# Second batch's scores stored ahead in DRAM, and the first batch's softmax divided after the product with V

## The chip, the cores and the metric

The kernel runs on one core of a Trainium2 chip. The metric is device time in microseconds: 1224.6 us, the median of three runs (1224.48 to 1224.6).

## The reference, cut to what matters

Attention over 4 batches, 8 heads, 576 tokens, head dimension 64, where each query keeps its 32 largest scores; then two MLPs of width 512 and hidden width 2048 over the 2304 tokens. Q, K, V and the result are float32, the MLP weights 64-bit; the kernel works with float32 operands, most of them split into a high and a low part.

```python
scores = scale * np.matmul(q, k.transpose(0, 1, 3, 2))
kth = np.partition(scores, -top_k, axis=-1)[..., -top_k:-top_k + 1]
scores = np.where(scores >= kth, scores, -1e9)
attn = np.exp(scores - max); attn = attn / (np.sum(attn) + 1e-09)
x = np.matmul(attn, v)              # 2304 x 512 after the heads are joined
x = np.square(np.maximum(x @ w_in, 0)) @ w_out
h = x @ w_in2; out = np.maximum(0.01 * h, h) @ w_out2
```

## The kernel before, in words

**Units and tiles.** The tokens of a batch are cut into units (UNITS): batch 0 into 256, 256 and 64 tokens, batches 1 to 3 into 256 and 320 each. For each of the four head pairs a unit gives tiles of 128 query rows by 576 keys: 144 tiles, 36 a batch, worked on in 72 pairs. The order is batch 0 (tiles 0 to 35), batch 1 (36 to 71: the 256-token unit up to 51, then the 320-token one), then batches 2 and 3 (72 to 143).

**One tile.** Scores (L278): 2 or 4 matmuls for each of two halves of 288 keys, each half evicted by ScalarE (L279). VectorE finds the 32 largest in four MAX8 (L800) with three MATCH_REPLACE8 between (L802). ScalarE and GpSimd drop what lies below (L297, L298), ScalarE takes exp with its row sum (L302), GpSimd and VectorE form the reciprocal `rc` (L306, L307), and ScalarE multiplies the tile by it (`norm`, L311). TensorE transposes the tile (`pt_main` L316, `pt_left` L329 for the last 64 keys), ScalarE evicts, and TensorE multiplies with V. Batch 0 (the units below NATIVE = 3) does this in plain float32 (`av`, L377); the others, for which `split(uh)` is true, with a high and a low part of the transposed tile (PTs, VT, L321, L322, L388). `x_out` (L397 on) writes the high and low part of the result into the MLP's input (L405, L408).

**MLP blocks.** The tokens go through the MLP in blocks of 512, 256, 384, 512, 256 and 384. Block 0 is the first two units, block 1 needs the first unit of batch 1, block 2 all of batch 1, block 3 the first units of batches 2 and 3. Blocks 0 to 3 run both layers as soon as they are ready. Block 0 also converts the weights, which come as 64-bit words: two ScalarE copies (L485, L486), two VectorE operations (L490, L491), a high part (L495) and a low part on GpSimd (L498), and a store to DRAM (L506, L507). Later blocks load the converted weights (L514, L515).

**Scores made ahead.** For a batch in EARLY (2 and 3) the scores are not made just before they are used. They are made during the first batch, into `stage` tiles through PSUM tiles `sp`, and stored to DRAM (`sd`, L282); `load_s` (L286) brings a tile back 24 slots before its pair starts. Their K is split by GpSimd (L117, L240: `st["i"]` is 99 there, so `split_hi` never picks ScalarE, as it does for batches 0 and 1, L115), their Q by ScalarE or GpSimd and GpSimd (L257). The K, Q and `stage` tiles lie in a pool `ahead`, the PSUM tiles in `stage_psum`; both are closed by `open_mlp`, and the MLP's own pools take that memory and those banks.

**What sets the order.** The work is emitted by slots, 16 to a pair of tiles. In each slot stand VectorE's next top-k instruction, the functions that `at(slot, ...)` put there, and a share of MLP matmuls: `rate` is a block's groups of three matmuls over the slots until the next block is ready; what is left when the next block is ready is emitted before that block. Direct scores stand 30 slots ahead of their pair (DLEAD). The ahead scores are spread over the slots of FILL, 2 to 245. Block 0 is ready at slot 274, block 1 at 434. The framework's scheduler keeps each engine's instructions in an order near that of emission and puts in the semaphores; each engine then runs its own list in order, and SP issues all loads and stores but those of the result.

Of the kernel before, what the change touches and what calls it, by code (L numbers as in the profile page):

```python
# [8 lines left out]
F = mybir.dt.float32  # L9
R = mybir.dt.float32r  # L10
U = mybir.dt.uint32
AF = mybir.ActivationFunctionType
OP = mybir.AluOpType
# [23 lines left out]

SPILL = 128

NATIVE = 3  # L40

EARLY = (2, 3)
FILL = (2, 245)
KPB = 2
NST = 3
SDB = 2
# [24 lines left out]
def topk_attention_moe_moe2_kernel(  # L71
# [11 lines left out]
    D = v.shape[-1]  # L83
    P = 128
# [8 lines left out]
    PE, ACT, DVE, POOL, SP = nc.tensor, nc.scalar, nc.vector, nc.gpsimd, nc.sync  # L93
# [9 lines left out]
    ident = const.tile([P, P], F, tag="ident", name="ident")  # L103
# [23 lines left out]
    for u in units:  # L127
        for hp in range(NHP):
            n = u["n"]
            uh = dict(u=u, hp=hp, n=n, b=u["b"], first=(u["t0"] == 0), ti=len(tiles), idx=len(uhs),  # L130
                      c0=P * (hp % 2) if n == 64 else 0)
# [14 lines left out]
    def direct(uh):  # L146
        return uh["b"] not in EARLY

# [3 lines left out]
    def split(uh):  # L152
        return uh["u"]["i"] >= NATIVE

# [5 lines left out]
    for i in range(4):  # L160
        x = const if i < 2 else ahead
# [10 lines left out]
    spill = const.tile([P, NHP, SPILL], F, tag="spill", name="spill")  # L172
    early_ctx = ExitStack()
    early = early_ctx.enter_context(tc.tile_pool(name="early", bufs=1))
    PT = early.tile([P, 5, 640], F, tag="PT", name="PT")
    late = {}

    def open_mlp():
# [4 lines left out]
    def open_late():  # L183
        early_ctx.close()
        late["pool"] = ctx.enter_context(tc.tile_pool(name="late", bufs=1))
        late["PT"] = late["pool"].tile([P, 9, 640], R, tag="PTs", name="PTs")

    events = {}

    def at(slot, fn, *a):  # L190
        events.setdefault(slot, []).append((fn, a))
# [4 lines left out]
    def load_k(b, hp, st):  # L196
        if b in EARLY:
            KT[b, hp] = ahead.tile([P, 2, S], R, tag="KTa", name="KTa", bufs=KPB)
        else:
            KT[b, hp] = pool.tile([P, 2, S], R, tag="KT", name="KT", bufs=4)  # L200
        x = ahead if b in EARLY else pool
        st["k"] = x.tile([P, 2, S], F, tag="kraw", name="kraw", bufs=1 if b in EARLY else KRB)
        SP.dma_start(st["k"], k[b, hp])
# [109 lines left out]
    def pt_main(t):  # L313
# [5 lines left out]
        if split(t["uh"]):  # L319
            pts = late["PT"]  # L320
            ACT.activation(pts[:, 0:4, c:c + P], x, AF.Copy)  # L321
            DVE.tensor_tensor(pts[:, 4:8, c:c + P], x, pts.bitcast(F)[:, 0:4, c:c + P], op=OP.subtract)  # L322
        else:
            ACT.activation(PT[:, 0:4, c:c + P], x, AF.Copy)

    def pt_left(pr):
# [8 lines left out]
        for t, c, o, m in groups:  # L335
            if split(t["uh"]):
                pts = late["PT"]
                ACT.activation(pts[0:64, 8, c:c + m], ps[0:64, o:o + m], AF.Copy)
                DVE.tensor_tensor(pts[64:128, 8, c:c + m], ps[0:64, o:o + m], pts.bitcast(F)[0:64, 8, c:c + m],  # L339
                                  op=OP.subtract)  # L340
            else:
                ACT.activation(PT[0:64, 4, c:c + m], ps[0:64, o:o + m], AF.Copy)


    blocks = []
    g = 0
# [6 lines left out]
    def block_x(blk):  # L353

        if "x" not in blk:
            i = SETS[blk["idx"]]
            m = max(x["n"] for x in blocks if SETS[x["idx"]] == i)
            if i == 2:
                ts = [pool.tile([P, 2, m], R, tag="wraw", name="x2", bufs=WRB) for _ in range(NK)]
                blk["x"] = [(t[:, 0], t[:, 1]) for t in ts]  # L360
            else:
                xpool = late["mlp"] if i else pool
                ts = [xpool.tile([P, NK, m], R, tag=f"x{c}{i}", name=f"x{c}{i}", bufs=1) for c in "hl"]
                blk["x"] = [(ts[0][:, c], ts[1][:, c]) for c in range(NK)]
        return blk["x"]

    def av(uh, hs, i):
# [6 lines left out]
        for m in range(3 * i, min(3 * i + 3, len(order))):  # L374
            h, j = order[m]
            np_ = P if j < NJ else LEFT
            PE.matmul(ps, lhsT=vt[0:np_, j, h * D:h * D + P], rhs=PT[0:np_, j, uh["c0"] + h * n:uh["c0"] + h * n + n],  # L377
                      start=m == 0, stop=m == len(order) - 1)
# [17 lines left out]
    def x_out(uh, hs):  # L396
        g0, n, hp = uh["u"]["g0"], uh["n"], uh["hp"]  # L397
        blk = blocks[cur["fill"]]
        end = blk["g0"] + blk["n"]
        m = min(n, end - g0)  # L400
        xh, xl = block_x(blk)[hp]
        c = g0 - blk["g0"]
        r = slice(hs[0] * 64, hs[-1] * 64 + 64)
        x = uh["xf"] if split(uh) else uh["avb"]
        ACT.activation(xh[r, c:c + m], x[r, 0:m], AF.Copy)  # L405
        if m < n:
            ACT.activation(spill[r, hp, 0:n - m], x[r, m:n], AF.Copy)
        (POOL if split(uh) else DVE).tensor_tensor(xl[r, c:c + m], x[r, 0:m], xh.bitcast(F)[r, c:c + m],  # L408
                                                   op=OP.subtract)
        if hp == NHP - 1 and hs[-1] == 1 and g0 + n >= end:  # L410
            ready.append(blk)
            cur["fill"] += 1
            if m < n:
                nxt = blocks[cur["fill"]]
                nxt["spilled"] = n - m
                if n - m == nxt["n"]:
                    ready.append(nxt)
                    cur["fill"] += 1
# [200 lines left out]
    def score_slot(ti):  # L619
        return 16 * (ti // 2) - DLEAD + 5 * (ti % 2)  # L620
# [5 lines left out]
    for uh in uhs:  # L626
        b, hp, i = uh["b"], uh["hp"], uh.get("di")
        z = score_slot(uh["ti"])
# [10 lines left out]
        if (b, hp) not in vdone or split(uh) and VTB < NHP:  # L639
            assert not uh["u"]["i"] < NATIVE <= units[max(x["i"] for x in units if x["b"] == b)]["i"]  # L640
            vdone.add((b, hp))
# [36 lines left out]
    for n, key in enumerate(keys):  # L678
# [10 lines left out]
        if n + 1 < len(keys):  # L689
# [4 lines left out]
            m = len(later) // (len(ks) + 1)  # L694
# [4 lines left out]
    for _ in range(2):  # L699
        at(FILL[0] - 1, request)  # L700
    done = 0
    for w, fn, args in fill:
        at(FILL[0] + (FILL[1] - FILL[0]) * done // total, fn, *args)
        done += w

    pairs = []
    for p in range(NPAIRS):
        pr = dict(t=tiles[2 * p:2 * p + 2], p=p)
        pairs.append(pr)
        z = 16 * p  # L710
        for i, t in enumerate(pr["t"]):
            if direct(t["uh"]):
                at(z - DLEAD + 5 * i, scores, t, 0)
                at(z - DLEAD + 2 + 5 * i, scores, t, 1)
            else:
                at(z - LEAD + i, load_s, t)
            if i == 0:
                at(z + 14, shifts, pr)
            at(z + 14 + i, drop, pr, i)
            at(z + 16 + i, expo_sum, pr, i)  # L720
            at(z + 20 + i, norm, pr, i)
            at(max(z + 20 + 3 * i, z + 21 + i), pt_main, t)
        at(z + 18, recip, pr)
        at(z + 26, pt_left, pr)
    rslot = [None] * len(blocks)

    def rmark(uh, z):
        if uh["hp"] == NHP - 1:
            e = uh["u"]["g0"] + uh["n"]
            for blk in blocks:  # L730
                if rslot[blk["idx"]] is None and blk["g0"] + blk["n"] <= e:
                    rslot[blk["idx"]] = z

    for uh in uhs:
        if split(uh):
            za, z = 16 * (uh["lastA"] // 2) + 30, 16 * (uh["last"] // 2) + 30
            at(za, av_split, uh, 0)
            at(z + 2, av_split, uh, 1)
            z += 4
            at(z, x_out, uh, (0, 1))  # L740
            rmark(uh, z)
            continue
        apart = uh["n"] == 320 and uh["ti"] % 2 == 0
        for hs in ((0,), (1,)) if apart else ((0, 1),):
            z = 16 * (uh["lastA"] // 2 if hs == (0,) else uh["last"] // 2) + 30
            nq = 2 * len(hs)
            for i in range(nq):
                at(z + i, av, uh, hs, i)
            at(z + nq, x_out, uh, hs)
        z += nq  # L750
        if uh["u"]["i"] == NATIVE - 1 and uh["hp"] == NHP - 1:
            at(z, open_late)
        rmark(uh, z)
# [30 lines left out]
    last = max(events)  # L784
    while slot <= last:
        p, i = divmod(slot, 16)
        if slot >= 0 and p < NPAIRS:
            pr = pairs[p]
# [6 lines left out]
            x = i % 2  # L795
            t = pr["t"][x]
            m8 = pr["m8"]
            r = i // 4
# [77 lines left out]
```

## Time and profile before

| | value |
|---|---|
| median of three runs | 1224.6 us |
| profiled execution: time, span | 1220.92 us, 1219.1 us |
| PE busy (weight loads) | 1139.2 us, 93% (996.5 us, 82%) |
| DVE busy | 946.1 us, 78% |
| ACT busy | 924.7 us, 76% |
| POOL busy | 721.0 us, 59% |
| DMA packets, mean rate | 323.24 MB, 265 GB/s |
| last chain of waits | PE 33%, DVE 3%, ACT 1% of the span |

PE is TensorE, PEld its weight loads, DVE VectorE, ACT ScalarE, POOL GpSimd, SP the engine that issues DMAs. A share of the span is a mean over stages whose limits differ, so the profile is best read by stage: before block 0's MLP, during it, and after. A group of instructions can show more busy time together than its engine, since the next one starts before the last has ended. An idle time is put down to what came last before it ended.

### The profile page before, as it was taken

To read this page: it belongs to the slowest core of one execution; us is meant where nothing else is said; L and a number is where in the kernel's file an instruction comes from. 1 tells how busy PE (TensorE), PEld (TensorE's weight loads), DVE (VectorE), ACT (ScalarE), POOL (GpSimd) and SP (SyncE) were. 2 spreads that over 40 slices of the span, in tenths; PEclk is the share of its full clock that TensorE was granted. 3 is DMA by queue.
4 is the path that set the end of the run, shared out by engine and by line. 5 is a ranking of instruction groups with operands and counts; after the bars stand their busy time and mean duration, and the time that the engine had idled before them with its cause. 6 is when DMAs were issued, how large, how long until landed. Compare 5 with 4: busy or idle time off the path is not lost. (4 is left out here: it accounts for less than half of the span.)

```text
span 1219.1 us, 20275 instructions
## 1 busy us (share of the span) xinstructions
PE 1139.2 (93%) x6352; PEld 996.5 (82%) x6352; DVE 946.1 (78%) x1944; ACT 924.7 (76%) x2031; POOL 721.0 (59%) x856
## 2 busy tenths in 40 slices
PE   4888887999889999999999999999999999999998
PEld 3676665787667879988999897788788899999997
DVE  7999998767998899999999999999999910110122
ACT  6999999989999998887878787777777764334322
POOL 8979795666789885467656685455476732004300
PEclk9889988999999999999999999999999999999999
DMA  9746557789889878989988788667666579779974
GB/s 311 225 169 207 182 183 269 263 279 314 300 294 326 299 265 272 309 267 373 367 290 290 247 286 280 203 235 238 196 229 222 197 257 364 264 251 332 361 254 136
DMA packets 110522, 323.24 MB, mean 265 GB/s; under 512 B 17488, under 2 KB 25680, under 8 KB 110416
## 3 DMA queue, kind: packets, MB, share of 16 engines
q1 hardware_dynamic: 107776, 317.24, 76.1%
q10 hardware_dynamic: 2640, 4.72, 1.1%
q8 instruction: 51, 0.84, 0.3%
q14 instruction: 55, 0.45, 0.1%
HBM read 254.54 MB, written 67.37 MB: 264 GB/s over the span
## 5 line engine op out<-in xcount | busy, mean ns | idle before, releaser
L552 PE MATMUL h<-xh,wi 128*128 128x512 f32 (+2 forms) x1280 | 350.0, 345 | 6.1 <-ACT gb L570 2.3
L800 DVE MAX8 m<-w 128x8 f32<-128x576 f32 x432 | 312.8, 747 | 1.7
L552 PEld LDWEIGHTS h<-xh,wi 128*128 128x128 f32 x1280 | 227.7, 191 | 33.2 <-ACT xh L603 3.9
L573 POOL TENSOR_TENSOR gl<-ga,gh 128x512 fp32r<-128x512 f32 (+2 forms) x160 | 162.9, 1018 | 124.5 <-ACT gh L572 44.5
L298 POOL TENSOR_TENSOR e<-s,e 128x576 f32<-128x576 f32 x144 | 203.3, 1432 | 42.1 <-ACT e L297 39.7
L802 DVE MATCH_REPLACE8 w<-m,w 128x576 f32<-128x576 f32 x288 | 213.4, 743 | 0.7
L552 PE MATMUL h<-xl,wi 128*128 128x512 f32 (+2 forms) x640 | 208.5, 343 | 2.8 <-DVE xl L604 2.7
L590 PE MATMUL acc<-gh,wo 128*128 128x512 f32 (+2 forms) x768 | 155.0, 341 | 1.8 <-ACT gh L572 1.7
L592 PE MATMUL acc<-wo,gh 128*128 128x512 f32 x576 | 151.6, 398 | 3.2 <-ACT gh L572 3.2
L571 POOL TENSOR_TENSOR ga<-ga,gb 128x512 f32<-128x512 f32 (+2 forms) x80 | 81.4, 1018 | 114.2 <-ACT gb L570 113.9
L590 PEld LDWEIGHTS acc<-gh,wo 128*128 128x128 f32 x768 | 124.6, 188 | 12.9 <-ACT gh L572 3.0
L552 PEld LDWEIGHTS h<-xl,wi 128*128 128x128 f32 x640 | 122.1, 192 | 15.7 <-DVE xl L604 4.7
L572 ACT ACTIVATE gh<-ga 128x512 fp32r<-128x512 f32 (+2 forms) x192 | 100.6, 524 | 34.3 <-POOL ga L571 22.8
L800 DVE MAX8 m<-s 128x8 f32<-128x576 f32 x144 | 104.7, 748 | 23.5 <-ACT s L279 22.2
L592 PEld LDWEIGHTS acc<-wo,gh 128*128 128x128 f32 x576 | 103.8, 188 | 23.3 <-ACT gh L572 5.0
L302 ACT ACTIVATE e<-e,kf 128x576 f32<-128x576 f32 x144 | 112.8, 784 | 10.4 <-POOL e L298 9.6
L297 ACT ACTIVATE e<-s,kf 128x576 f32<-128x576 f32 x144 | 106.5, 782 | 16.8 <-POOL kf L290 14.9
L311 ACT ACTIVATE e<-e,rc 128x576 f32<-128x576 f32 x144 | 104.8, 781 | 11.6 <-DVE rc L307 11.3
L562 ACT ACTIVATE ga<-h 128x512 f32<-128x512 f32 (+2 forms) x96 | 47.0, 490 | 80.6 <-PE h L552 80.2
L802 DVE MATCH_REPLACE8 w<-m,s 128x576 f32<-128x576 f32 x144 | 107.0, 743 | 0.6
L316 PE MATMUL att<-ident,e 128*128 128x128 f32 x576 | 88.6, 285 | 10.0 <-ACT e L311 4.5
L278 PE MATMUL sp<-KTa,q 128*128 128x288 f32 x320 | 68.8, 350 | 25.6 <-ACT stage L279 21.2
(89 smaller groups left out, 2129.8 us busy)
## 6 DMA issues: line engine op xcount, KB each, us to landing
wi<-wd SPq DMA_DIRECT2D x160, 512.0 KB, 5.2
wo<-wd SPq DMA_DIRECT2D x160, 512.0 KB, 5.2
wraw<-in_w_dram SPq DMA_DIRECT2D x64, 512.0 KB, 5.8
sd<-stage SPq DMA_DIRECT2D x72, 288.0 KB, 3.0
s<-sd SPq DMA_DIRECT2D x72, 288.0 KB, 4.9
wd<-wi SPq DMA_DIRECT2D x32, 512.0 KB, 6.1
wd<-wo SPq DMA_DIRECT2D x32, 512.0 KB, 5.6
kraw<-in_k_dram SPq DMA_DIRECT2D x16, 576.0 KB, 4.3
```

Of the source, the lines that this page charges most:

```text
L297: ACT.activation(e, x, AF.Relu, bias=pr["kf"][:, i:i + 1], scale=-FAR)
L298: cur["pool"] = POOL.tensor_tensor(e, x, e, op=OP.subtract)
L302: ACT.activation(e, e, AF.Exp, bias=pr["nb"][:, i:i + 1], scale=0.125, accum_out=pr["sum"][:, i:i + 1])
L311: ACT.activation(e, e, AF.Copy, scale=pr["rc"][:, i:i + 1])
L316: PE.transpose(ps[:, j * P:(j + 1) * P], t["e"][:, j * P:(j + 1) * P], ident)
L552: PE.matmul(h[:, 0:n], lhsT=wi[:, w, c * P:(c + 1) * P], rhs=x[c][y][:, 0:n], start=cnt == 0, stop=cnt == 3 * NK - 1)
L572: ACT.activation(gh[:, 0:n], a[:, 0:n], AF.Copy)
L573: (DVE if j >= GLD else POOL).tensor_tensor(gl[:, 0:n], a[:, 0:n], gh.bitcast(F)[:, 0:n], op=OP.subtract)
L590: PE.matmul(acc[c][:, 0:n], lhsT=wo[:, w, cs], rhs=g[:, 0:n], start=first, stop=last)
L592: PE.matmul(acc[c], lhsT=g[:, cs], rhs=wo[:, w, :], start=first, stop=last)
L800: cur["dve"] = DVE.max(out=m8[:, x, 8 * r:8 * r + 8], in_=t["s"] if r == 0 else t["w"])
L802: cur["dve"] = DVE.match_replace(out=t["w"], in_to_replace=m8[:, x, 8 * r:8 * r + 8], in_values=t["s"] if r == 0 else t["w"], imm_value=NEG)
```

## The change

Batch 1 joins EARLY: its 36 tiles' scores are made in the same stretch as those of batches 2 and 3, 108 tiles instead of 72, stored and loaded back. FILL now ends at slot 268. Batch 0 no longer calls `norm`: the un-normalised exponentials are transposed and multiplied with V, and `pt_left` also transposes the reciprocals (a column of 128, broadcast to 128x128) into the free half of its PSUM bank and copies them to an SBUF tile `rb`, whose columns are tokens. `x_out` of batch 0 multiplies the product by `rb` on VectorE into a tile `xn`, copies the high part as before, and takes the low part on GpSimd instead of VectorE. PT shrinks from 640 to 512 columns. The last hunk's new condition is true for the same units as the old one: those of batch 0 have 256 or 64 tokens.

```diff
-EARLY = (2, 3)
-FILL = (2, 245)
+EARLY = (1, 2, 3)
+FILL = (2, 268)
-    PT = early.tile([P, 5, 640], F, tag="PT", name="PT")
+    PT = early.tile([P, 5, 512], F, tag="PT", name="PT")
@@ pt_left
+        segs = []
+        for i, t in enumerate(pr["t"]):
+            uh, n = t["uh"], t["uh"]["n"]
+            if split(uh):
+                continue
+            c = 2 * P + i * P
+            PE.transpose(ps[:, c:c + P], pr["rc"][:, i:i + 1].to_broadcast([P, P]), ident)
+            if "rb" not in uh:
+                uh["rb"] = early.tile([P, 256], F, tag="rb", name="rb", bufs=2)
...
+        for uh, h, t0, m, c in segs:
+            r = slice(h * D, h * D + D)
+            ACT.activation(uh["rb"][r, t0:t0 + m], ps[r, c:c + m], AF.Copy)
@@ x_out
-        x = uh["xf"] if split(uh) else uh["avb"]
+        if split(uh):
+            x = uh["xf"]
+        else:
+            x = early.tile([P, 256], F, tag="xn", name="xn", bufs=1)
+            DVE.tensor_tensor(x[r, 0:n], uh["avb"][r, 0:n], uh["rb"][r, 0:n], op=OP.mult)
-        (POOL if split(uh) else DVE).tensor_tensor(xl[r, c:c + m], x[r, 0:m], xh.bitcast(F)[r, c:c + m],
+        POOL.tensor_tensor(xl[r, c:c + m], x[r, 0:m], xh.bitcast(F)[r, c:c + m],
@@ main plan
-            at(z + 20 + i, norm, pr, i)
+            if split(t["uh"]):
+                at(z + 20 + i, norm, pr, i)
-        apart = uh["n"] == 320 and uh["ti"] % 2 == 0
+        apart = uh["n"] > P and uh["n"] % P and uh["ti"] % 2 == 0
```

`segs` joins neighbouring stretches: a pair of a 256-token unit gives one copy of 64x256, a pair of the 64-token unit four of 64x64.

## Rows read from the trace of the kernel before

**Rows 1.** Windows: us; PE, PEld, DVE, ACT, POOL busy us (count); PEclk, DMA share, GB/s
```profile
0.00:211.00 211.00, 163.20 (x815) 130.53 (x815) 195.82 (x417) 190.95 (x479) 170.46 (x240) 0.90 0.67 221
211.00:456.00 245.00, 231.02 (x1133) 188.89 (x1133) 200.93 (x379) 230.56 (x473) 191.48 (x188) 0.99 0.85 292
456.00:761.00 305.00, 295.28 (x1913) 277.43 (x1913) 301.62 (x637) 244.34 (x547) 192.20 (x240) 0.99 0.87 298
761.00:1219.00 458.00, 449.73 (x2491) 399.67 (x2491) 247.69 (x514) 258.83 (x536) 166.85 (x189) 0.99 0.72 249
```

**Rows 2.** Timeline: start us, us, engine, line, out<-in; where the stages meet
```profile
207.36 0.43 ACT L279 ACTIVATE stage<-sp 128x288 f32<-128x288 f32 x1
208.58 0.86 PE L552 MATMUL h<-xh,wi 128*128 128x512 f32 x3
210.66 0.43 ACT L405 ACTIVATE xh<-att 128x256 fp32r<-128x256 f32 x1
451.77 0.37 ACT L405 ACTIVATE xh<-xf 128x192 fp32r<-128x192 f32 x1
455.70 0.64 ACT L607 ACTIVATE y<-acc 128x512 f32<-128x512 f32 x1
760.79 0.41 ACT L405 ACTIVATE xh<-xf 128x256 fp32r<-128x256 f32 x1
```

**Rows 3.** Waits, 211 to 456: engine line waited for: us, times, longest
```profile
DVE wc L490 <- ACT att L486: 22.7, 14, 3.3
DVE m L800 <- ACT s L279: 14.3, 10, 2.9
```

**Rows 4.** Groups by line, 211 to 456: busy us, mean ns, idle before
```profile
L311 ACT ACTIVATE e<-e,rc 128x576 f32<-128x576 f32 x22 | 16.0, 787 | 0.0
L279 ACT ACTIVATE s<-att 128x288 f32<-128x288 f32 x42 | 17.2, 417 | 0.1
L278 PE MATMUL att<-KT,q 128*128 128x288 f32 x94 | 20.4, 309 | 2.1 <-DVE xf L394 1.1 <-DVE PTs L322 0.7
```

**Rows 5.** Groups by line, 0 to 211 (before block 0's MLP)
```profile
L279 ACT ACTIVATE stage<-sp 128x288 f32<-128x288 f32 x144 | 54.1, 431 | 4.0 <-PE sp L278 3.3
L311 ACT ACTIVATE e<-e,rc 128x576 f32<-128x576 f32 x34 | 25.2, 806 | 0.0
L115 ACT ACTIVATE KT<-kraw 128x576 fp32r<-128x576 f32 x16 | 10.2, 687 | 5.2 <-DMA kraw<-in_k_dram 5.2
L342 ACT ACTIVATE PT<-att 64x256 f32<-64x256 f32 x16 | 6.4, 402 | 0.0
L257 POOL TENSOR_TENSOR q<-qraw,q 128x256 fp32r<-128x256 f32 (+2 forms) x59 | 41.5, 716 | 2.0 <-ACT q L115 0.7
L117 POOL TENSOR_SCALAR q<-qraw 128x256 fp32r<-128x256 f32 (+1 forms) x32 | 13.6, 432 | 12.1 <-PE sp L278 7.9 <-DMA qraw<-in_q_dram 3.6
L117 POOL TENSOR_SCALAR KTa<-kraw 128x576 fp32r<-128x576 f32 x16 | 10.5, 672 | 0.1
```

**Rows 6.** Timeline: runs of one line on ACT and on PE
```profile
186.43 1.03 ACT L279 ACTIVATE stage<-sp 128x288 f32<-128x288 f32 x3
197.69 2.37 PE L278 MATMUL sp<-KTa,q 128*128 128x288 f32 x10
```

**Rows 7.** Groups by line and shape, whole span
```profile
L316 PE MATMUL att<-ident,e 128*128 128x128 f32 x576 | 88.6, 285 | 10.0 <-ACT e L311 4.5 <-ACT PT L324 2.5 <-DVE wc L491 2.2
L408 POOL TENSOR_TENSOR xl<-xf,xh 128x256 fp32r<-128x256 f32 x12 | 8.9, 743 | 9.9 <-ACT xh L405 9.9
L408 DVE TENSOR_TENSOR xl<-att,xh 128x256 fp32r<-128x256 f32 x8 | 3.3, 410 | 0.0
```

**Rows 8.** Waits of SP's queue: 0 to 211, then 211 to 456
```profile
SPq L282 <- ACT stage L279: 78.1, 51, 5.2
SPq L462 <- ACT att L486: 75.9, 41, 4.5
```

**Rows 9.** DMA: a window with the highest rate, columns as in rows 1
```profile
549.00:579.00 30.00, 28.92 (x197) 26.34 (x196) 29.76 (x63) 23.58 (x55) 21.91 (x30) 1.00 1.01 372
```

More of the change, by code (lines that the diff above doesn't have):

```diff
@@ L342, in pt_left @@
                 ACT.activation(PT[0:64, 4, c:c + m], ps[0:64, o:o + m], AF.Copy)
+        segs = []
[7 more added lines that the diff above has]
+                uh["rb"] = early.tile([P, 256], F, tag="rb", name="rb", bufs=2)
+            r0 = (t["i"] - uh["ti"]) * P
+            for h in range(2):
+                a, e = max(r0, h * n), min(r0 + P, h * n + n)
+                if a >= e:
+                    continue
+                last = segs[-1] if segs else None
+                if last and last[0] is uh and last[1] == h and last[2] + last[3] == a - h * n:
+                    last[3] += e - a
+                else:
+                    segs.append([uh, h, a - h * n, e - a, c + a - r0])
+        for uh, h, t0, m, c in segs:
+            r = slice(h * D, h * D + D)
+            ACT.activation(uh["rb"][r, t0:t0 + m], ps[r, c:c + m], AF.Copy)
     blocks = []
@@ L403, in x_out @@
         r = slice(hs[0] * 64, hs[-1] * 64 + 64)
-        x = uh["xf"] if split(uh) else uh["avb"]
+        if split(uh):
+            x = uh["xf"]
+        else:
+            x = early.tile([P, 256], F, tag="xn", name="xn", bufs=1)
+            DVE.tensor_tensor(x[r, 0:n], uh["avb"][r, 0:n], uh["rb"][r, 0:n], op=OP.mult)
         ACT.activation(xh[r, c:c + m], x[r, 0:m], AF.Copy)
```

## The prediction

> **What bounds the kernel now.** I first cut the span into stages at the points where MLP blocks start, and read each engine's busy time in each [rows 1]. The cuts come from the timeline [rows 2]: the last high part of block 0's input is written at 210.66 us; the last one of block 1's at 451.77, with block 0's last result tile beginning eviction at 455.70; the last one of block 3's at 760.79. So: stage A, 0 to 211 (batch 0's attention and the scores made ahead); B, 211 to 456 (block 0's MLP and the weight conversion, over the first tiles of batch 1); C, 456 to 761 (blocks 1 and 2); D, 761 to 1219 (blocks 3 to 5).
>
> The reader is to see that the tightest engine changes [rows 1]. In A VectorE has 195.8 us of 211 and ScalarE 191.0, GpSimd 170.5, TensorE 163.2. In B VectorE falls to 200.9 of 245, while ScalarE (230.6) and TensorE (231.0) both stand at 94%. In C VectorE is at 301.6 of 305. In D TensorE is at 449.7 of 458. The waits of B say who is late [rows 3]: VectorE stood 22.7 us for a ScalarE copy of the weight conversion and 14.3 us for scores that ScalarE had not yet evicted. So ScalarE sets B's pace, with TensorE close.
>
> One rule sharpens this. TensorE's busy time in B ties with ScalarE's, but its weight loads are busy only 188.9 of 245 us [rows 1]. The Trainium skill, Perfetto Trace Analysis, section Identifying the Most-Contended Engine, says to judge TensorE's headroom by weight-load time, not matmul time, because pipelined matmuls mislead; by that, ScalarE alone bounds B. If TensorE bound it, the gain in B below would be 21.7 us instead of 17.5.
>
> **Stage B, what leaves it.** Of batch 1's 72 score evictions, 42 fall in B, 17.2 us of ScalarE; the other 30 are 5 in A and 25 in C by the same count. In B also run 22 norms in 16.0 us [rows 4]; 4 are the last tiles of batch 0 (32 to 35) and go, 4 x 0.727 = 2.9 us. Added there: the 8 small copies of `rb` of the 64-token unit; no row has that shape, the 64x256 copy at 0.402 [rows 5] bounds one from above and 0 from below; I take 0.2 each, 1.6 us. ScalarE: -17.2 - 2.9 + 1.6 = -18.5 us, as sums over lines. Neighbouring instructions overlap: three evictions in a run take 1.03 us, 0.34 each against 0.431 alone [rows 5, 6], a factor of 0.8. At 0.8 to 1.0 that is 14.8 to 18.5 us of engine time; I take 16.5. At the same 94% it shortens B by 16.5/0.94 = 17.5 us. TensorE loses 94 score matmuls, 20.4 us [rows 4], so it doesn't take over. VectorE has 44 us in hand; it and TensorE together forbid more than about 24 us (20.4/0.94 is 21.7, and a little for the waits on scores). From below: the transfers, a rival further down, could leave 6.
>
> **Stage A, what comes in.** ScalarE: 67 more evictions (72 less the 5 already in A) at 0.34 to 0.431 are +23 to +29 us; 34 norms go, -25.2; K of batch 1 is no longer split by ScalarE, half of 16 instructions at 10.2 us, -5.1; the `rb` copies of 16 pairs at 0.402 (the same shape, evicted for PT) +6.4 [rows 5, 6]. Sum -1 to +5 on 191.0. The late division thus pays for the evictions.
>
> GpSimd: the high part of batch 1's K, 8 x 0.672 = 5.4; the 11 low parts of Q not yet in A (59 of 70 are), 11 x 0.716 = 7.9; 8 more high parts (32 of 40), 8 x 0.432 = 3.5; 8 low parts of `x_out` that come from VectorE, 8 x 0.743 = 5.9 [rows 5, 7]. Sum +22.7 on 170.5, that is 193 of 211. This is the tight one: its drop (L298) frees score buffers, behind which ScalarE's evictions and VectorE wait, and its splits feed the scores.
>
> TensorE: 150 more score matmuls (160 less 10 in A), 0.237 each in a run of ten [rows 6], +36 us; 32 transposes of `rc` between 0.154 (88.6/576) and 0.285 each [rows 7], +5 to +9. Together 163.2 + 43 = 206 of 211 if nothing packs tighter. The granted clock in A is 0.90 on average against 0.99 in B [rows 1], so TensorE still has slower stretches there that fuller work may lift; I count nothing for it.
>
> VectorE: 8 multiplications at about the price of the subtractions that leave (0.410, also one PSUM and one SBUF operand) [rows 7]: nothing. On the path to block 0's start lies one of them, at 0.41 us, and a wait behind up to one top-k step; the norm's ScalarE step leaves the same path (0.74, 25.2/34), so I count zero. The low part now queues on GpSimd behind a drop or two; the MLP's first matmuls need the high parts first, and that covers it.
>
> SP: 31 stores and as many K and Q loads as batch 1 had in B move into A. Its queue already stood 78.1 us in A for staged evictions, with weight loads behind [rows 8]; more such waits delay what is queued, but weights are asked for 80 slots before use.
>
> So A has one engine near the same load and two pushed to 92 and 97%. Its length is bounded by 0 (everything hides under VectorE's 196 us) and by about +24 us (GpSimd's or half of TensorE's addition all shows). One thing makes lateness count at once: the last staged eviction began at 207.36 and block 0's first matmul at 208.58 [rows 2]. The MLP takes over the memory and banks of the ahead scores, so block 0 cannot start before the last of 108 tiles is out. And FILL now ends 6 slots before block 0 instead of 29. I take +7, nearer to the ScalarE sum than to the outer bound.
>
> **Stages C and D.** C loses 25 evictions and their matmuls, but VectorE's 301.6 of 305 stays [rows 1]: at most 3.4 us come off; I take 0.5. MLP block 2 may start earlier and then waits at C's end for block 3's tokens. D holds only batches 2 and 3, which don't change: 0.
>
> **Transfers.** 31 of 36 tiles' stores land in A, whose DMA share is 0.67 [rows 1]. In B some 21 tiles of 295 KB are loaded back, 6.2 MB, less about 1.3 MB of batch 1's Q that moves out. B moved 245 us x 292 GB/s = 71.5 MB; 76.4 MB in 228 us are 335 GB/s. A window of C ran at 372 GB/s with a share of 1.01, VectorE busy 29.8 of 30 us [rows 9], so I let this fit. SP's queue in B waited 75.9 us for weight buffers [rows 8]; a score load in front of a weight load waits for a drop, and was asked for 1.5 pairs ahead.
>
> **Sum.** +7 - 17.5 - 0.5 = -11 us on the profiled execution, whose time is 1220.9 (span 1219.1): 1209.9. The median of the runs lies 3.7 us above that execution; so 1213.6.
>
> **Rivals.**
> 1. A doesn't grow: ScalarE's sum of about zero rules, and C gives its 3.4. For it: ScalarE's addition in A is about zero, and VectorE, the busiest there, gets none. Against: what GpSimd and TensorE take on. -17.5 - 3.4 = -21: 1204.
> 2. GpSimd and TensorE at their limit delay the ahead scores, and block 0 waits for the last of them. A +24, B -17.5: +6.5, 1231. It decides once block 0's first matmul comes later than about 229 us, 18 to 20 us after today. For it: the 1.2 us between the last staged eviction and that matmul. Against: GpSimd's 40 idle us in A.
> 3. B is held by transfers. The weight loads share the queue and the engines with score loads, and B shrinks by 6 only: +7 - 6 = +1, 1225.6. For it: share 0.85 already. By the Trainium skill, SBUF — State Buffer, section A bandwidth-pool intuition that's wrong (but worth ruling out), memory gives one core about 358 GB/s; 335 would be 94% of that. Against: the trace's 372 is above this figure.
> 4. The evictions and matmuls leave B but it doesn't shrink, because the slots tie VectorE's tiles to MLP groups that don't change. Then the time is 1224.6 + 7, as in rival 2; the two share its chance.
>
> **How the numbers follow.** Forecast 0.50 (1207 to 1220), rival 1 0.20, rivals 2 and 4 0.18, rival 3 0.12. A measurement can tell about 0.2%, 2.5 us, from no change. Faster: nearly all of the forecast and rival 1, 0.69; same: 0.02 of the forecast and most of rival 3, 0.10; slower: 0.21. The range holds eight in ten with 1199 below (rival 1 with 5 us more from B) and 1232 above. The likeliest case's own is 1207 to 1220.
>
> **What would show it.** Right: 108 norms instead of 144, 216 staged evictions, 108 score loads; block 0's last high part at 213 to 224; from there to block 0's last result 223 to 233 us instead of 245; ScalarE still the busiest there, VectorE no longer waiting for scores; block 3's last high part near 750; D unchanged at 458. Wrong: block 0 starting after 229, or B longer than 239, or VectorE's idle time in C above 10 us because score loads come late.

## The result, and the profile after

The changed kernel is slower: 1242.1 us against 1224.5, a ratio of 1.0146 [1.0119, 1.0172]. The prediction was 1213.6, faster; the time lies outside its range. Its profiled execution has a span of 1240.0 us, 20.9 more than before. Ratios here and below are of fast executions; one of the ten executions of run e9 (further down), at 2800 us, is left out.

Busy time by stage, cut as [rows 1] but at the changed kernel's own borders (us; PE, PEld, DVE, ACT, POOL busy with counts; granted clock, DMA share, GB/s), and two windows inside the first stage:

```profile
0.00:255.00 255.00, 202.95 (x1044) 164.70 (x1044) 233.09 (x494) 211.09 (x556) 201.63 (x285) 0.89 0.76 257
255.00:495.00 240.00, 221.74 (x1040) 179.39 (x1041) 181.75 (x347) 212.66 (x419) 180.68 (x172) 0.96 0.87 302
495.00:789.00 294.00, 287.19 (x1843) 269.29 (x1843) 289.77 (x613) 235.07 (x515) 189.07 (x236) 0.99 0.90 317
789.00:1240.00 451.00, 442.61 (x2465) 393.88 (x2464) 237.64 (x492) 252.87 (x524) 161.65 (x183) 1.00 0.74 251
180.00:210.00 30.00, 21.03 (x94) 16.50 (x94) 26.85 (x56) 26.69 (x65) 24.59 (x31) 0.80 0.98 344
210.00:237.00 27.00, 21.90 (x86) 19.15 (x84) 26.88 (x58) 18.28 (x45) 16.43 (x22) 0.53 0.90 349
```

The borders come from its timeline: the last high part of block 0's input, the last ahead evictions, the first MLP matmul, the last results of block 0, the last high part of block 3's input, the last results of block 2. They answer to [rows 2].

```profile
202.45 0.42 ACT L433 ACTIVATE xh<-xn 128x256 fp32r<-128x256 f32 x1
253.38 0.71 ACT L280 ACTIVATE stage<-sp 128x288 f32<-128x288 f32 x2 [0.24 <-DMA sd<-stage]
254.34 0.71 ACT L280 ACTIVATE stage<-sp 128x288 f32<-128x288 f32 x2 [0.24 <-DMA sd<-stage]
255.10 2.08 PE L580 MATMUL h<-xh,wi 128*128 128x512 f32 x8 [0.71 <-ACT stage L280]
494.26 1.06 ACT L635 ACTIVATE y<-acc 128x512 f32<-128x512 f32 x2
778.21 0.42 ACT L433 ACTIVATE xh<-xf 128x256 fp32r<-128x256 f32 x1
789.05 0.62 ACT L635 ACTIVATE y<-acc 128x512 f32<-128x512 f32 x1
```

Block 0's input was complete at 202.45, 8 us earlier than before. Its MLP began at 255.10, 46.5 us later than before (208.58), and the matmul says for what it waited: an eviction of an ahead tile. Stage A, to that start, is 255 us long; B, to block 0's last result, 239 (247 before); C, to block 2's, 295 (301); D 451 (462). All after A is shorter by 25 us, and A is longer by 46. TensorE is busy 221.7 of 240, 287 of 294 and 443 of 451 us in B, C and D: once the MLP has begun, TensorE has little slack. From the first MLP matmul to the end, before and after:

```profile
208.58:1219.10 1010.52, 978.06 (x5546) 866.97 (x5544) 752.52 (x1532) 736.15 (x1559) 552.94 (x618) 0.99 0.80 274
255.10:1240.00 984.90, 951.54 (x5344) 842.56 (x5344) 709.16 (x1450) 700.55 (x1455) 531.39 (x591) 0.99 0.82 283
```

TensorE is busy 26.5 us less there and idle some 33 us in both. So what the change gains behind the start is TensorE work that came before it: batch 1's scores, and six tiles of attention that VectorE had begun by then (44 instead of 38). The 46 us paid in front of it are more.

In the last 26 us of A (from 229) ScalarE runs nothing but ahead evictions, with gaps. Who waited, 180 to 256 us (total us, times, longest), and the share of the chain of waits by line over 180 to 300 us:

```profile
PEld sp L279 <- ACT stage L280: 20.6, 23, 3.4
PE sp L279 <- ACT stage L280: 13.9, 12, 3.2
ACT stage L280 <- DMA sd<-stage: 7.1, 13, 1.9
```

```profile
by line: DMA sd<-stage 18.9%; PE h L580 14.2%; PE att L401 13.2%; PE acc L618 10.8%; ACT stage L280 6.5%; PE sp L279 6.5%; issue 4.5%; DVE m L829 2.8%; DVE w L831 2.5%; ACT wc L513 2.5%; POOL e L299 2.0%; ACT e L303 2.0%; DVE wc L518 1.5%; 
```

TensorE waits for a PSUM tile that ScalarE has not emptied, ScalarE for a staging tile whose store to DRAM has not landed: the store is the largest item of the chain, 18.9%. From 210 to 237 us ScalarE is busy 18.3 of 27 us.

The edit did what it says (whole span; busy us, mean ns, idle before). These answer to [rows 4, 5]: 108 norms, 216 ahead evictions, 24 copies of `rb` at 0.33 us, 12 multiplications at 0.35.

```profile
L280 ACT ACTIVATE stage<-sp 128x288 f32<-128x288 f32 x216 | 80.5, 426 | 23.6 <-PE sp L279 12.4 <-DMA sd<-stage 7.1 <-issue 2.5
L312 ACT ACTIVATE e<-e,rc 128x576 f32<-128x576 f32 x108 | 77.8, 770 | 14.0 <-DVE rc L308 13.8
L366 ACT ACTIVATE rb<-att 64x256 f32<-64x256 f32 (+1 forms) x24 | 8.0, 332 | 0.6 <-PE att L351 0.3
L432 DVE TENSOR_TENSOR xn<-att,rb 128x256 f32<-128x256 f32 (+1 forms) x12 | 4.2, 352 | 11.5 <-POOL xl L436 9.9 <-ACT rb L366 1.4 <-PE att L401 0.2
```

In B, VectorE's waits are others than in [rows 3]: scores loaded back late, the conversion still, and one stall of 9.9 us where the multiplication of the 64-token unit waited for the single `xn`, whose reader waited for block 1's input tile, which lies in the memory that the ahead scores had just left. That stall began at 248 us, 7 us before B: the gate held VectorE too.

```profile
DVE m L829 <- DMA s<-sd: 17.0, 9, 4.2
DVE wc L518 <- ACT wc L513: 16.0, 7, 3.9
DVE xn L432 <- POOL xl L436: 9.9, 1, 9.9
257.96 0.22 DVE L432 TENSOR_TENSOR xn<-att,rb 128x64 f32<-128x64 f32 x1 [9.94 <-POOL xl L436]
```

### The profile page after: what moved, and what is told of

Same layout as the page of the kernel before. It is cut to its first block, busy times and chain, and to the rows that moved or that the text cites. A ratio compares the mean times of both kernels' runs of the same rounds, so it can differ in the third digit from the quotient of the medians.

```text
span 1240.0 us, 20589 instructions
## 1 busy us (share of the span) xinstructions
PE 1154.5 (93%) x6388; PEld 1007.3 (81%) x6388; DVE 942.2 (76%) x1944; ACT 911.7 (74%) x2011; POOL 733.0 (59%) x876
## 4 chain that ended last, share of the span: by engine, by line
PE 56%; DVE 12%; ACT 8%; DMA 5%; POOL 4%; issue 4%; ACTq 0%; POOLq 0%; DVEq 0%
PE h L580 23%; PE acc L618 12%; PE acc L620 11%; DVE m L829 5%; DVE w L831 4%; PE att L412 3%; PE att L317 3%; DMA s<-sd 2%; DMA sd<-stage 2%; PE att L401 2%; DVE PTs L323 1%; POOL gl L601 1%; POOL ga L599 1%; ACT stage L280 1%; ACT e L303 1%
## 5 line engine op out<-in xcount | busy, mean ns | idle before, releaser
L580 PE MATMUL h<-xh,wi 128*128 128x512 f32 (+2 forms) x1280 | 345.4, 342 | 6.8 <-ACT ga L590 3.5
L580 PE MATMUL h<-xl,wi 128*128 128x512 f32 (+2 forms) x640 | 206.6, 340 | 3.2 <-DVE xl L632 3.0
L618 PE MATMUL acc<-gh,wo 128*128 128x512 f32 (+2 forms) x768 | 158.7, 347 | 6.7 <-ACT gh L600 6.7
L618 PEld LDWEIGHTS acc<-gh,wo 128*128 128x128 f32 x768 | 127.2, 191 | 18.8 <-ACT gh L600 7.8
L279 PE MATMUL sp<-KTa,q 128*128 128x288 f32 x480 | 101.6, 347 | 26.5 <-ACT stage L280 22.8
L279 PEld LDWEIGHTS sp<-KTa,q 128*128 128x128 f32 x480 | 79.4, 216 | 40.8 <-ACT stage L280 34.3
L317 PE MATMUL att<-ident,e 128*128 128x128 f32 x576 | 92.4, 284 | 14.4 <-ACT e L303 8.3
```

The source lines that it names most:

```text
L279: PE.matmul(ps[:, 0:HALF], lhsT=l, rhs=r, start=i == 0, stop=i == len(mm) - 1)
L317: PE.transpose(ps[:, j * P:(j + 1) * P], t["e"][:, j * P:(j + 1) * P], ident)
L580: PE.matmul(h[:, 0:n], lhsT=wi[:, w, c * P:(c + 1) * P], rhs=x[c][y][:, 0:n], start=cnt == 0, stop=cnt == 3 * NK - 1)
L618: PE.matmul(acc[c][:, 0:n], lhsT=wo[:, w, cs], rhs=g[:, 0:n], start=first, stop=last)
```

## The experiments

Theory, **gate**: block 0's MLP takes the memory and banks of the ahead scores; 108 tiles through three staging tiles end at 255 us; from a late start TensorE has no slack, so the start sets the end. Rivals: the late division itself costs; working and loading batch 1's tiles costs; ScalarE, not TensorE, sets B. Times are medians; the stages come from each profile, which is of one execution and can lie some us from the median (e1's 4 above it, e5's 5, that of before 4 below).

| kernel | last ahead eviction | first MLP matmul | block 0's last result | span | span less first matmul |
|---|---|---|---|---|---|
| before | 207.4 | 208.6 | 455.7 | 1219.1 | 1010.5 |
| changed | 254.3 | 255.1 | 494.3 | 1240.0 | 984.9 |
| e1 | 189.1 | 189.9 | 453.6 | 1218.8 | 1028.9 |
| e2 | 265.8 | 267.3 | 504.7 | 1253.9 | 986.6 |
| e3 | 189.6 | 196.3 | 446.8 | 1223.7 | 1027.4 |
| e4 | 237.0 | 239.3 | 475.8 | 1221.1 | 981.8 |
| e5 | 245.7 | 246.5 | 482.1 | 1250.1 | 1003.6 |
| e6 | 203.2 | 205.0 | 450.4 | 1218.4 | 1013.4 |
| e9 | 206.6 | 220.2 | 461.1 | 1217.4 | 997.2 |
| e10 | 227.8 | 230.6 | 475.4 | 1221.3 | 990.7 |
| e11 | 187.4 | 222.0 | 475.1 | 1237.4 | 1015.4 |
| e12 | 238.0 | 239.0 | 477.9 | 1232.9 | 993.9 |

(us; a run of evictions is given by its start. Where block 0's last input was late, only three MLP matmuls ran ahead of it: the fourth came at 211.1 before, 204.8 in e1, 200.9 in e3, 207.7 in e6, 224.0 in e9 and 223.6 in e11.)

**e1, the late division alone.**

```diff
-EARLY = (1, 2, 3)
-FILL = (2, 268)
+EARLY = (2, 3)
+FILL = (2, 245)
```

> The changed kernel with batch 1's scores made late again (EARLY of two batches, FILL to 245): the late division alone. Theory, gate: block 0's MLP cannot start before the last ahead tile is out, and with 72 tiles that is near 200 to 207 us; the first MLP matmul comes at 200 to 207 and the time is 1216 to 1223. Rival, the late division costs by itself (one xn buffer, a VectorE step and GpSimd's queue on the path to the MLP's input): first MLP matmul after 212, time above 1227.

1216.5 us, 0.9938 [0.9915, 0.9961] of before: it does not cost, it gains 8 us. The timeline shows the start early, and block 0's last input at 204.36, 6 us sooner than in [rows 2]:

```profile
189.11 0.70 ACT L280 ACTIVATE stage<-sp 128x288 f32<-128x288 f32 x2
189.87 1.07 PE L580 MATMUL h<-xh,wi 128*128 128x512 f32 x3 [1.05 <-ACT stage L280]
204.36 0.41 ACT L433 ACTIVATE xh<-xn 128x256 fp32r<-128x256 f32 x1
```

The first matmul comes 10 us before I expected it, on the input of the first three head pairs. But only three matmuls run then; the next ones wait for the last input:

```profile
204.82 2.50 PE L580 MATMUL h<-xh,wi 128*128 128x512 f32 x5 [0.54 <-ACT xh L433]
```

So block 0 really starts 6 us sooner than before (204.8 against 211.1) and ends 2 us earlier. The two profiled executions hardly differ (spans of 1218.8 and 1219.1 us), so they do not show where the 8 us of the medians come from.

**e2, batch 1 ahead alone.**

```diff
-EARLY = (2, 3)
-FILL = (2, 245)
+EARLY = (1, 2, 3)
+FILL = (2, 268)
-    PT = early.tile([P, 5, 640], ...
+    PT = early.tile([P, 5, 512], ...
```

> The kernel before with batch 1 added to the ahead scores and FILL to 268, norms kept, PT at 512 columns. Theory, gate: the last of 108 ahead tiles comes at 255 us or later, since 34 norms are back on ScalarE: 257 to 270; time 1241 to 1250. Rival, the late division costs: time below 1236.

1254.5 us, 1.0243 [1.022, 1.0267], a little above the expected range; the first matmul at 267.3, inside it. The loss is batch 1's; the late division gave 12 us of it back.

**e3, batches 1 and 2 ahead, batch 3 late.**

```diff
-EARLY = (1, 2, 3)
-FILL = (2, 268)
+EARLY = (1, 2)
+FILL = (2, 245)
```

> The changed kernel with batches 1 and 2 made ahead and batch 3 made late, FILL to 245: 72 tiles ahead, batch 1 among them. Theory, gate: first MLP matmul at 200 to 210, as with 72 tiles of batches 2 and 3. It also tests the stage with block 0's MLP alone, without the late start: if my term of 17.5 us there was right, from the first MLP matmul to block 0's last result it is 224 to 233 us; if loading batch 1's scores back beside the weights takes the gain, 238 or more. Batch 3's scores now lie in the last stage, which TensorE fills: +15 to +35 us there. Time 1220 to 1240.

1226.1 us, 1.0015 [1.0001, 1.0029]. The start, 196.3, is 4 us before its range, but B is 250.5 us, not 224 to 233: my term for B fails even without a late start. VectorE began tile 60 at 440 us instead of 460 and did some 25 tiles in the stage instead of 21: the stage took in more attention rather than end sooner. VectorE's longest wait in it is for scores loaded back, 16.3 us, so the expectation's other case (the loading takes the gain) is not ruled out. Stage D grew by 12 us.

**e4, five staging tiles.**

```diff
-NST = 3
+NST = 5
```

> The changed kernel with five staging tiles instead of three. If the end of the ahead scores (228 to 255 us, where ScalarE does nothing else) waits for stores to land, the last ahead eviction comes 5 to 12 us earlier and the time is 1233 to 1239. If it is set by where the work stands in the order or by TensorE, nothing moves: 250 to 256 and 1239 to 1245.

1222.2 us, 0.9969 [0.9953, 0.9985]: 20 us less than the changed kernel, more than I had expected, and the start 16 us earlier. The last evictions and the first matmul, and the windows that answer to the changed kernel's above:

```profile
236.99 2.28 ACT L280 ACTIVATE stage<-sp 128x288 f32<-128x288 f32 x6 [0.20 <-PE sp L279]
239.32 0.96 PE L580 MATMUL h<-xh,wi 128*128 128x512 f32 x3 [0.54 <-ACT stage L280]
```

```profile
180.00:210.00 30.00, 23.03 (x108) 17.89 (x108) 29.34 (x63) 28.66 (x69) 26.69 (x32) 0.82 1.01 375
210.00:237.00 27.00, 24.95 (x108) 22.09 (x109) 27.00 (x58) 21.80 (x58) 15.52 (x21) 0.63 0.98 377
239.00:476.00 237.00, 218.71 (x1037) 176.08 (x1038) 189.82 (x362) 211.63 (x420) 180.93 (x172) 0.98 0.87 305
```

ScalarE is busy 21.8 of 27 us from 210 to 237 instead of 18.3, and DMA moves 377 GB/s instead of 349. The waits of 180 to 256 us, with five tiles:

```profile
PEld sp L279 <- ACT stage L280: 10.0, 14, 1.8
ACT stage L280 <- DMA sd<-stage: 0.7, 1, 0.7
```

ScalarE's wait for stores, 7.1 us in the changed kernel, is nearly gone. The three staging tiles were a main part of the delay.

**e5 and e6, the kernel before with two and with five staging tiles.**

```diff
-NST = 3
+NST = 2
```

> The kernel before with two staging tiles instead of three: same work, 72 tiles ahead, the norms kept. Theory, gate: the last ahead eviction slips to 225 to 260 us and the first MLP matmul follows it within 3 us; where that comes later than 235, the span is the first matmul plus 980 to 988, as in the three kernels that started at 239, 255 and 267. Rival (the loss lies in loading and working batch 1's tiles, not in the start): the start may slip, but the time stays within 1222 to 1229.

1246.5 us, 1.0179 [1.0162, 1.0196]. This kernel has nothing of the change, only a later end of the ahead scores (timeline):

```profile
245.73 0.71 ACT L279 ACTIVATE stage<-sp 128x288 f32<-128x288 f32 x2 [1.35 <-DMA sd<-stage]
246.49 2.87 PE L552 MATMUL h<-xh,wi 128*128 128x512 f32 x7 [1.87 <-ACT stage L279]
```

So the late start alone costs as much as the change did. The 980 to 988 us that I expected behind it are 1003.6, 17 to 22 more than in the kernels that start late with batch 1 ahead (e2, e4, the changed one). Some 5 us of that may be this execution's, which took that much more than the median; the rest is about what making batch 1's scores ahead is worth once the start is late.

```diff
-NST = 3
+NST = 5
```

> The kernel before with five staging tiles: control for e4. Theory, gate: the ahead scores end earlier, but block 0's own input (210.7 us before) then decides, so 1220 to 1227. If more staging tiles help whatever the start does: below 1217.

1222.0 us, 0.9989 [0.9977, 1.0002], the same: five staging tiles help where the ahead scores hold the start, and not before the change.

**e7 and e8, what sets B.** Both from e4. e7 leaves out the products with the low part of block 0's input in the first matrix of each layer; e8 moves the high part of the weights to VectorE.

```diff
+                if j == 0:
+                    mm = [m for m in mm if not m[2]]
```

> The changed kernel with five staging tiles, block 0's first-matrix products without the low part of their input (128 of 768 matmuls of 512 columns left out, both layers; 128 x 0.2325 = 30 us of TensorE). If TensorE sets block 0's stage, it shrinks from 236 us (first matmul to last result) to 206 to 218. If ScalarE or transfers set it: 230 or more.

```diff
-            ACT.activation(w[:, 0, :], c, AF.Copy)
+            DVE.tensor_scalar(w[:, 0, :], c, 1.0, 1.0, op0=OP.mult, op1=OP.mult)
```

> The changed kernel with five staging tiles and the 64 high parts of the weights (0.64 us each, some 38 us in block 0's stage) made by VectorE instead of ScalarE. If ScalarE sets block 0's stage, as I predicted, it shrinks from 236 us to 200 to 222 and the time falls below 1212. If TensorE sets it: 230 to 240 and 1216 to 1228.

From first matmul to block 0's last result e7 takes 219.5 us (1211.5 in all, 0.9903 [0.9888, 0.9918]), e8 231.9 (1224.6, 0.9998 [0.9986, 1.0011]), e4 236.5. The windows of e7, then e8, to be read against e4's third line above:

```profile
238.00:458.00 220.00, 192.69 (x873) 153.65 (x874) 175.80 (x335) 203.53 (x403) 176.54 (x167) 0.94 0.90 321
```

```profile
242.00:474.00 232.00, 217.35 (x1024) 174.07 (x1024) 222.83 (x410) 182.83 (x357) 183.78 (x171) 0.98 0.89 311
```

With 26 us less of TensorE the stage lost 17 us, just short of the range; with 29 us less of ScalarE it lost 5, and the whole run nothing. TensorE sets B with five staging tiles. e8 alone would not prove it, since VectorE took the work on and is busy 222.8 of 232 there. Of e7's 17 us the whole run kept 11 (1211.5 against 1222.2): fewer tiles of attention were done in the stage (17.5 instead of 20), and the last stage took 9 us more (459.5 against 450.0). No run tried the same on the kernel before.

**e9 and e10, a PSUM bank more for the ahead scores.** e9 with five staging tiles, e10 with three:

```diff
-SDB = 2
-SPB = 3
+SDB = 1
+SPB = 4
```

> The changed kernel with five staging tiles, and one PSUM bank moved from the first batch's own scores to the ahead ones (SPB 4, SDB 1). If TensorE and ScalarE wait for free banks, the ahead scores flow faster: last ahead eviction at 200 to 222 us, first MLP matmul at most 3 us later or with block 0's last input (202). Then the span is the larger of that start plus 980 to 988 and the attention's own path: 1195 to 1210. If banks don't matter: first matmul at 235 to 243, 1217 to 1226.

> The same move of one bank with the changed kernel's three staging tiles: which of the two sets the rate of the ahead scores. Both needed: first matmul 235 to 250, time 1220 to 1236. Banks alone enough: first matmul below 225, time below 1212.

e9: 1221.3 us, 0.9964 [0.9947, 0.9981], 11 above the range that I expected; e10: 1223.5, 0.9992 [0.9975, 1.0008]. In e9 the ahead scores end at 206.6, 48 us before the changed kernel's, but now block 0's own input is late, which the moved bank made (VectorE's wait for its scores, 100 to 225 us, was 0.7 in e4):

```profile
206.58 0.73 ACT L280 ACTIVATE stage<-sp 128x288 f32<-128x288 f32 x2
220.21 0.96 PE L580 MATMUL h<-xh,wi 128*128 128x512 f32 x3
223.58 0.40 ACT L433 ACTIVATE xh<-xn 128x256 fp32r<-128x256 f32 x1
```

```profile
DVE m L829 <- ACT s L280: 12.8, 12, 3.1
```

The gate is gone and another wait stands there: the last input at 223.6 instead of 203.3 in e4. e10's start, 230.6, lies between its two cases. Banks and staging tiles both slow the ahead scores; how much of e10's gain is the bank and how much the slower first batch, which leaves them room, the runs do not separate.

**e11 and e12, 88 tiles ahead.** e11 is e9 with batch 1's 320-token unit late, e12 is e4 with batch 3's. K is kept apart for the late unit; the core:

```diff
-        return uh["b"] not in EARLY
+        return uh["b"] not in EARLY or uh["b"] == 1 and not uh["first"]
...
-        return uh["b"] not in EARLY
+        return uh["b"] not in EARLY or uh["b"] == 3 and not uh["first"]
```

> As e9, but of batch 1 only the 256-token unit (16 of its 36 tiles) is made ahead, its 320-token unit late as before: 88 tiles ahead. The last ahead eviction comes below 205 and block 0's input decides: first matmul at 196 to 206. Batch 1's other 20 tiles put some 90 score matmuls (about 11 us of TensorE) back behind the start: 1198 to 1212, against e9 by the start it wins less these 11 us.

> The changed kernel with five staging tiles and 88 tiles ahead: the 20 tiles a head pair at a time of batch 3's 320-token unit are made late, in the last stage, where VectorE has room and TensorE does not. Theory, gate: the last ahead eviction at 205 to 225 us and the first MLP matmul within 3 us; the span is the larger of that plus 980 to 988 plus some 7 us (e3 paid 13 for 36 tiles in the last stage) and the attention's path: 1203 to 1217, faster than e4. Rival: the last stage pays more than the start gains: above 1222.

Both expectations were wrong. e11: 1239.8 us, 1.013 [1.011, 1.015]; the ahead scores ended at 187, the first batch's input held the start as in e9 (222), and what follows took 1015 us instead of 997, 18 more where I had reckoned 11. e12: 1234.8 us, 1.0079 [1.0048, 1.0111]; with 20 tiles fewer the ahead scores still ended at 238, since the last head pair's K came late: GpSimd waited for its load and split it only then (e12's timeline):

```profile
225.97 1.30 POOL L118 TENSOR_SCALAR KTa<-kraw 128x576 fp32r<-128x576 f32 x2 [2.64 <-DMA kraw<-in_k_dram]
230.09 2.79 POOL L242 TENSOR_TENSOR KTa<-kraw,KTa 64x576 fp32r<-64x576 f32 x2
```

So the number of tiles is not the only thing that sets their end; the loads in front of them count too. In its last stage (from block 2's last result) e12 lost 11 us against e4 where I had reckoned 7.

Of the versions that do all the work with batch 1 ahead, the best (e4, e9) are 0.3 to 0.4% faster than the kernel before; e1, without it, is 0.6% faster, at 1216.5.

## Why the prediction was wrong

**Stage A, the step that failed.** "So A has one engine near the same load and two pushed to 92 and 97%", and from it "+7, nearer to the ScalarE sum than to the outer bound". Measured +46.5, beyond the outer bound of +24 as well. The step took the stage's length from sums of busy time and gave the ahead scores' path through three staging tiles and three PSUM banks, and its wait for stores to land, no term. The sums do not show the delay: to 211 us ScalarE is busy 181.8 us, GpSimd 178.0 and TensorE 166.8, all below what I had summed, because the work was not done by then. 162 of the 216 ahead evictions had started. What held the ahead scores back is in the main a chain through few buffers: matmuls, an eviction, a store that lands, a tile free again. Two more staging tiles brought its end from 254.3 to 237.0 (e4), a moved bank besides to 206.6 (e9). ScalarE's other work counts too: with the 34 norms kept the end is at 265.8 (e2). The trace of before held a sign. The last ahead eviction began at 207.36, while FILL had put it at slot 245, and VectorE passed that slot at some 162 us by its tiles: 45 us late in a stage where ScalarE was 90% busy. I had used that eviction only to see that block 0 cannot start before it. But in the kernel before this lag was mostly not the staging tiles': five of them took 4 us off it (e6, 203.2), the late division 18 (e1, 189.1).

Two counts in the sums were wrong and change little: 38 norms were taken off, 34 in A and 4 in B, where batch 0 has 36 (1.5 us of ScalarE), and all 36 of batch 1's stores are new in A, not 31.

**The rival that came.** Rival 2 is what happened in its second half (the MLP waits for the last ahead tile) and nearly by its point of decision: it set 229 us; with 984 us behind a late start, 1219.1 is reached at 235. Its first half, GpSimd and TensorE at their limit, is not: they were busy 178.0 and 166.8 of 211 us. Its price was too small, +24 for A, since it too was worked out from the engines' busy time.

**Stage B.** "ScalarE sets B's pace, with TensorE close" and -17.5: measured -8 (247 to 239), and 236.5 and 237.4 in e4 and e2. ScalarE lost 21 us (232.6 to 211.7), a little more than I had summed, and the stage did not follow: in e4, where it was tried, TensorE set it (e7, e8). TensorE lost 20.4 us by the line's busy time, but only 12 in the windows between first matmul and last result (232.6 to 220.8). Why, no run separates: the score matmuls overlap with their neighbours, the rest of the work in the stage differs, and the granted clock was 0.96 instead of 0.99. Nor is the -8 shown to come from the scores that left: e5, which moves none, has a B of 235.6 us, and e3, which moves them and starts early, 250.5. The stages hold different amounts of attention besides: 21 tiles before, 19 in the changed kernel, 18 in e5, 25 in e3. The rule cited there from the Trainium skill (Perfetto Trace Analysis, section Identifying the Most-Contended Engine), weight-load time in place of matmul time, pointed the wrong way in e4: weight loads were busy 176.1 of 237 us, and TensorE was the limit all the same. The section names a second measure beside it, the share of peak matmul work, which the prediction left out.

**What held, and what else did not.** Stage C shrank by 6 us, where I had taken 0.5, and D by 11, where I had taken nothing. TensorE had less to do in both (26.5 us less behind the start, with the idle time as before): batch 1's late scores were gone from C, and the attention was further along when D began (110.5 tiles begun instead of 108). The late division pays: e1 and e2 put it at 8 and 12 us. That block 0's input came 8 us earlier is not its doing alone: e2, which keeps the norms, has it at 202.83. Transfers were not the main limit (rival 3): B moved 302 GB/s, and e4 377 in another window; but late score loads do appear as a wait of VectorE, 17 us in B. Whether the slots alone hold B (rival 4) stays open: e7 shortened it, but by taking out MLP groups, to which that rival ties the tiles, and e3, with 25 tiles and no shorter stage, looks like it.

## What to carry to other kernels

When work is moved to an earlier stage that has idle engines, ask first what must be finished before the next stage may start, and at what rate the chain of buffers behind that work runs; the engines' sums of busy time only give a lower bound. Compare where the program puts the last piece with when it ran: a lag there, already before the change, says that something else than the order sets the pace, and a run with more buffers or less work on one engine tells which. And settle which of two engines at 94% bounds a stage by taking work off one of them, not by a rule.

## What the runs showed of the hardware

From 205 to 235 us the changed kernel's TensorE had a granted clock of 0.50, the lower of its two levels (1.2 of 2.4 GHz); in the 25 us before it had been busy 16.9 us at 0.86.

```profile
180.00:205.00 25.00, 16.86 (x78) 12.99 (x78) 21.85 (x46) 21.83 (x53) 20.99 (x25) 0.86 0.97 343
205.00:235.00 30.00, 24.15 (x91) 21.22 (x92) 29.88 (x62) 21.60 (x52) 18.03 (x24) 0.50 0.93 353
```

Part of the late ahead scores ran in it, and no run separates what the clock cost them. e4's clock was 0.50 too from 210 to 230 us, so the earlier end there is not the clock's alone. And DMA moved 377 GB/s for 27 us in e4, stores and loads mixed, above the 358 that the Trainium skill, SBUF — State Buffer, section A bandwidth-pool intuition that's wrong (but worth ruling out), gives between memory and one core.
